# A convolution moved into four quarters of the TensorE array, with 56-token blocks, three-slot units and three PSUM banks for the front

## Chip, cores, metric

One core of a Trainium2 chip. The time is device microseconds (us) of one execution. Every experiment was timed beside the kernel before on the same chip, in the same rounds; different jobs got different chips, and that turned out to matter (the kernel before has a median of 725.5 us on one and 622.8 to 624.2 on three others). In the profile's lines PE is TensorE (PEld its weight loads), DVE VectorE, ACT ScalarE, POOL GpSimd and SP SyncE, which issues most of the loads; a q behind the name is that engine's sequencer, and L101 is line 101 of the kernel. "Ratio" is the mean time of one kernel's fast runs over that of the kernel before in the same rounds, so not quite the ratio of the medians quoted.

## The reference

```python
# x: 8 x 3584 x 192 fp32 (28,672 tokens); weight: 8 heads x 7 taps
w = softmax(weight)                                   # per head
y[t] = sum_k w[head, k] * x[t - 6 + k]                # causal, zero-padded per sequence
logits = y @ w_gate;  e = argmax(logits)              # 8 experts, top 1
g = softmax(logits)[e];  o = sigmoid(y @ w_output_gate)[e]
out = g * o * (relu(y @ w1[e]) @ w2[e])               # 192 -> 1024 -> 192
```

## The kernel before

Tokens go through in 16 units of 1,792. The *front* of a unit loads x, does the convolution as a matmul with a band matrix, transposes, computes the gate, and scatters the rows, sorted by expert, to a stream in HBM. The *slots* read 512 rows of one expert back (two transposing DMAs, xa and xb) and do the two expert matmuls. In the main loop unit u runs four slots while the front of unit u+2 is laid between them. The parts the change touches:

```python
BT = 112; KI = BT + 6                                  # block of 112 tokens, 118 rows with history
def load_x(u):
    ...
    nc.sync.dma_start(xt[0:BT, c0:NB, :], src(c0, NB - c0, 0, BT))      # 112 partitions
    nc.sync.dma_start(xt[BT:KI, c0:NB, :], src(c0, NB - c0, BT, KI))    # 6 partitions
...
def front_a(u):
    for h in range(H):                                 # one head a step, whole array
        pc = pft()
        nc.tensor.matmul(pc[0:BT, 0:NB * GH], band[0:KI, h, :], xt[0:KI, :, h*GH:(h+1)*GH], ...)
        evac(cv[0:BT, :, h*GH:(h+1)*GH], pc[...])
        yield
    if ahead and u + 2 < NU: xts[u + 2] = load_x(u + 2)
...
for u in range(U0, NU):                                # main loop
    while k < len(todo):                               # slots
        for q in range(4):
            pos = 4 * k + q
            if 0 <= 16*(u-U0) + pos - 4 < 16: load_w(1)      # expert weights, one piece
            ... s.first / front steps / prev.second ...
            if pos == 7 and u + 1 < NU: nxt = loads(u + 1)   # slot loads of the next unit
```

## Time and profile before

| | us |
|---|---|
| timed, median of 3 (range) | 719.81 (716.82 to 725.0) |
| the profiled execution (span) | 622.8 (621.1) |
| TensorE busy in that span | 575.6, 93% |
| a unit in the steady part | 36.7 |
| a full slot of 512 rows, TensorE alone | 5.65 |

TensorE is busy almost without a gap in the steady part (35.9 of the 36.6 us of a unit), so the span there is the sum of its work; the lines that show it are in the prediction. Two more lines of the page, in 40 equal slices of the span, are the granted TensorE clock in tenths, and the mean busy share of the 16 DMA engines in tenths.

```profile
PEclk9999989999999999999999999999999999989997
DMA  6999759993847365464635647354463425256631
```

### The profile page before, as it was taken

Reading aid. Unit: us, or ns where it says so; the run is one execution under the profiler, and the core shown is the slowest. Engines: PE = TensorE matmul, PEld = TensorE weight load, DVE = VectorE, ACT = ScalarE, POOL = GpSimd, SP = SyncE. Lnnn points to the kernel's source line nnn. Section 1 sums busy time; section 2 is a strip of 40 time slices with the busy share of each in tenths; the row PEclk is TensorE's granted clock in tenths of the full one; section 3 lists DMA queues with packets and bytes.
Section 4 is the critical chain, followed back from the end, with each engine's and each line's share of the span. In section 5 each row is a group of like instructions: output and inputs, shape, how many; then the busy total and the mean of one; then the engine's idle time right before and its main releaser. Section 6 shows DMA issues by size and latency. Waiting matters only on the chain.

```text
span 621.1 us, 13578 instructions
## 1 busy us (share of the span) xinstructions
PE 575.6 (93%) x4544; PEld 359.2 (58%) x4544; DVE 380.4 (61%) x1310; ACT 381.8 (61%) x638; POOL 403.5 (65%) x419
## 2 busy tenths in 40 slices
PE   3999689999999999999999999999999999989992
PEld 1555346665665756566565665666566665646561
DVE  7678664856739476584946658385674948526231
ACT  1677555675666656576575656667566666746761
POOL 1378538777766757576575766747576675775774
PEclk9999989999999999999999999999999999989997
DMA  6999759993847365464635647354463425256631
GB/s 159 203 198 258 184 112 195 157 254 109 194 115 154 128 119 173 109 182 98 164 110 115 177 103 187 88 133 142 114 180 95 103 90 110 80 124 129 186 107 37
DMA packets 162569, 88.13 MB, mean 142 GB/s; under 512 B 116766, under 2 KB 153793, under 8 KB 162497
## 3 DMA queue, kind: packets, MB, share of 16 engines
q1 hardware_dynamic: 131872, 43.92, 32.0%
q0 software_dynamic: 29728, 43.30, 26.5%
q8 instruction: 36, 0.59, 0.4%
q14 instruction: 37, 0.29, 0.2%
q10 hardware_dynamic: 896, 0.03, 0.1%
HBM read 35.92 MB, written 43.06 MB: 127 GB/s over the span
## 4 chain that ended last, share of the span: by engine, by line
PE 80%; DVE 7%; ACT 5%; DMA 4%; issue 2%; POOL 1%; ACTq 0%; SPq 0%; POOLq 0%; DVEq 0%
PE pyt L668 22%; PE pp L626 18%; PE pf L303 12%; PE pp L633 10%; PE pf L457 6%; PE pf L317 6%; PE pf L326 4%; ACT ht L646 3%; DVE ht L644 2%; PE pf L335 1%; ACT cv L291 1%; DMA out_dram<-y,oi 1%; DMA xb<-xcg_sorted 1%; DVE np L382 1%; DVE xrow L422 1%
## 5 line engine op out<-in xcount | busy, mean ns | idle before, releaser
L495 POOL DMA_INDIRECT out_dram<-y,oi x246 | 244.7, 995 | 121.4 <-ACT y L674 57.1
L646 ACT ACTIVATE ht<-pp 128x1024 f16<-128x1024 f32 (+1 forms) x189 | 182.9, 1001 | 57.7 <-PE pp L633 56.7
L668 PE MATMUL pyt<-wres,ht 128*128 128x192 f16 x1920 | 191.4, 246 | 0.0
L668 PEld LDWEIGHTS <-ht 128*128 128x128 f16 x1968 | 167.4, 98 | 24.4 <-issue 10.9
L475 POOL DMA_INDIRECT xcg_sorted<-xs,du x128 | 133.3, 1042 | 72.4 <-ACT xs L291 31.7
L644 DVE TENSOR_SCALAR ht<-pp 128x1024 f16<-128x1024 f32 (+1 forms) x63 | 75.4, 1198 | 73.6 <-PE pp L626 73.6
L303 PE MATMUL pf<-xt,band 118*112 118x384 f32 x256 | 104.9, 504 | 11.0 <-DMA wg<-n_moe_w_output_gate_dram 10.6
L626 PE MATMUL pp<-xa,wres 128*128 128x512 f16 x240 | 93.2, 388 | 4.9 <-DMA xa<-xcg_sorted 4.8
L626 PE MATMUL pp<-xb,wres 128*128 128x512 f16 x240 | 91.5, 381 | 2.2 <-DMA xb<-xcg_sorted 2.2
L291 ACT CAST xs<-pf 128x388 f16<-128x388 f32 x128 | 61.6, 485 | 49.7 <-PE pf L457 47.9
L674 ACT COPY y<-pyt 128x384 f32<-128x384 f32 x123 | 58.4, 475 | 36.2 <-PE pyt L668 33.5
L633 PE MATMUL pp<-xa,wres 64*128 64x512 f16 x240 | 73.1, 385 | 0.0
L633 PE MATMUL pp<-xb,wres 64*128 64x512 f16 x240 | 73.1, 385 | 0.0
L626 PEld LDWEIGHTS <-wres 128*128 128x128 f16 x480 | 33.8, 97 | 66.9 <-issue 62.7
L457 PE MATMUL pf<-xrow,pm 112*128 112x194 f16 x512 | 64.5, 247 | 7.4 <-ACT cv L291 4.0
L457 PEld LDWEIGHTS <-pm 112*128 112x128 f16 x512 | 44.9, 97 | 34.5 <-issue 12.3
L427 DVE TENSOR_SCALAR pm<-pos,pos 112x256 f16<-112x256 f16 x256 | 62.6, 305 | 0.0
L422 DVE TENSOR_TENSOR xrow<-cv,gs 112x384 f16<-112x384 f32 x121 | 61.9, 550 | 0.0
L303 PEld LDWEIGHTS pf<-xt,band 118*112 118x112 f32 x256 | 41.6, 182 | 26.5 <-DVE band L142 11.0
L293 DVE COPY cv<-pf 112x384 f32<-112x384 f32 x48 | 26.5, 551 | 42.9 <-PE pf L303 42.8
L291 ACT COPY cv<-pf 112x384 f32<-112x384 f32 x80 | 38.0, 478 | 21.6 <-PE pf L303 21.0
L317 PE MATMUL pf<-identf,cv 112*128 112x112 f32 x384 | 49.3, 259 | 0.7 <-ACT cv L291 0.7
(135 smaller groups left out, 432.2 us busy)
## 6 DMA issues: line engine op xcount, KB each, us to landing
xt<-in_x_dram SPq DMA_DIRECT2D x8, 1344.0 KB
xt<-in_x_dram SPq DMA_DIRECT2D x8, 1260.0 KB
out_dram<-y,oi POOLq DMA_INDIRECT x246
wres<-in_moe_w_dram POOLq DMA_DIRECT2D x8, 384.0 KB
wd<-wres SPq DMA_DIRECT2D x3, 768.0 KB
wres<-in_moe_w_dram POOLq DMA_DIRECT2D x8, 256.0 KB
xcg_sorted<-xs,du POOLq DMA_INDIRECT x128
xcg_sorted<-zrow SPq DMA_DIRECT2D x8, 256.0 KB
```

Of the source, the lines that this page charges most:

```text
L291: nc.scalar.copy(out=o, in_=i)
L303: nc.tensor.matmul(pc[0:BT, 0:NB * GH], band[0:KI, h, :], xt[0:KI, :, h * GH:(h + 1) * GH], start=True, stop=True)
L317: nc.tensor.matmul(pt[:, j * BT:(j + 1) * BT], cvf[0:BT, m * 2 * D + i * 128:m * 2 * D + (i + 1) * 128], identf[0:BT, 0:BT], is_transpose= ...
L422: nc.vector.tensor_tensor(out=xr[P, k:k + 2, 0:D], in0=cv[P, k:k + 2, :], in1=gs[P, k:k + 2].unsqueeze(2).to_broadcast([BT, 2, D]), op=ALU ...
L457: nc.tensor.matmul(ps[:, r * XW:(r + 1) * XW], pm[P, l, r * 128:(r + 1) * 128], xr[P, l * NG + i, :], start=(r == 0 and l == 0), stop=(r = ...
L475: i = nc.gpsimd.indirect_dma_start(out=xcg2, out_offset=bass.IndirectOffsetOnAxis(ap=du[:, i:i + 1], axis=0), in_=xs.rearrange("p r w -> p ...
L495: i = nc.gpsimd.indirect_dma_start(out=out, out_offset=bass.IndirectOffsetOnAxis(ap=oi[:, j:j + 1], axis=0), in_=y[:, j, :], in_offset=Non ...
L626: nc.tensor.matmul(pps[r][:, l, :], w[:, o2:o2 + 128], x, start=(r == 0), stop=(r == 1))
L633: nc.tensor.matmul(pps[r][:, l, :], w[p0:p0 + 64, c:c + 128], x[p0:p0 + 64], start=(r == 1), stop=(r == 0))
L644: nc.vector.tensor_relu(out=ht, in_=pps[r])
L646: nc.scalar.activation(out=ht, in_=pps[r], func=AF.Relu)
L668: nc.tensor.matmul(self.pp[:, o:o + D], self.ht[fc // 2][:, fc % 2, q * 128:(q + 1) * 128], self.w[:, w:w + D], start=(fc == 0 and q % 2 = ...
```

## The change

Its intent: take TensorE time away. A 64x64 quarter of the array gets a block of 56 tokens with 6 rows of history (62 partitions); four quarters multiply together. In five of the units three slots run instead of four, and the remaining rows go to slots picked at the end. The front gets three PSUM banks (PSUM is the memory that the kernel's matmuls write to: pf, pp and pyt in the profile's lines), the second matmul keeps one. Weights start earlier. The core (helpers, names and the rest of the placement cut):

```diff
-    BT = 112
-    KI = BT + PADL
+    BH = 56
+    KH = BH + PADL                 # 62
+    PT = 64 + BH                   # 120 partitions, 8 of them dead
@@ load_x
-        nc.sync.dma_start(xt[0:BT, c0:NB, :], src(c0, NB - c0, 0, BT))
-        nc.sync.dma_start(xt[BT:KI, c0:NB, :], src(c0, NB - c0, BT, KI))
+        nc.sync.dma_start(xt[0:KH, c0:NB, :], src(c0, NB - c0, 0))
+        nc.sync.dma_start(xt[64:64 + KH, :, :], src(NB, NB, 0))
@@ pools
-    ps_y bufs=2   ps_f bufs=2
+    ps_y bufs=1   ps_f bufs=3
@@ front_a
-        for h in range(H):
-            pc = pft()
-            nc.tensor.matmul(pc[0:BT, 0:NB * GH], band[0:KI, h, :], xt[0:KI, :, ...])
+        for h in range(0, H, 2):
+            pcs = [pft(), pft()]
+            for hh in range(2):
+                for r, c in ((0, 0), (1, 1), (0, 1), (1, 0)):
+                    nc.tensor.matmul(pcs[r][64*c:64*c+64, ...], band[64*r:64*r+KH, h+hh, :],
+                                     xt[64*r:64*r+KH, c*NG:(c+1)*NG, ...])
@@ plan
-        p = plan_half(u % 2, "a")                       # four experts a unit
+        n = 3 if u in (4, 6, 8, 10, 12) else 4 if u < NU - 1 else E
@@ weights
-    load_w(8)          # before the first front; 8 more in the prologue, 16 in the loop
+    load_w(12)         # much earlier; 4 + 16 in the loop
```

## The prediction

> **What bounds the kernel now.** I read the page first: engine shares, the 40 slices, the chain that ended last, then the timeline of TensorE in the steady part, then the chain in order of time, and last the DMA issues.
>
> ```profile
> span 621.1 us, 13578 instructions
> ## 1 busy us (share of the span) xinstructions
> PE 575.6 (93%) x4544; PEld 359.2 (58%) x4544; DVE 380.4 (61%) x1310; ACT 381.8 (61%) x638; POOL 403.5 (65%) x419
> ...
> PE 80%; DVE 7%; ACT 5%; DMA 4%; issue 2%; POOL 1%; ACTq 0%; SPq 0%; POOLq 0%; DVEq 0%
> ```
>
> TensorE is busy 93% and owns 80% of the chain; the others have a third of their time free. The timeline of TensorE in the middle shows why: no gaps, one stage following the other.
>
> ```profile
> 303.75 0.82 PE L303 MATMUL pf<-xt,band 118*112 118x384 f32 x2
> 304.41 0.50 PE L457 MATMUL pf<-xrow,pm 112*128 112x194 f16 x4
> ...
> 327.24 1.71 PE L326 MATMUL pf<-tt,wg 128*32 128x448 f32 x16
> 328.88 0.39 PE L626 MATMUL pp<-xa,wres 128*128 128x512 f16 x1
> ```
>
> The columns are start, length, engine, line. One head of the convolution (L303) holds TensorE from 303.75 to 304.41, so 0.65 us; a unit of 1792 tokens has 8, so 5.2 us. The gating matmuls of a unit (L326: four column tiles of 32, twice, fp32) take 1.64 us to the next stage. The chain in order of time gives the period: the same L326 piece stands at 290.65, 327.31 and 363.98.
>
> ```profile
> 290.65 1.64 PE pf L326 x16
> ...
> 327.31 1.64 PE pf L326 x16
> ...
> 363.98 1.64 PE pf L326 x16
> ...
> 537.41 1.32 PE pyt L668 x16
> ...
> 540.24 1.32 PE pyt L668 x16
> ...
> 543.07 1.32 PE pyt L668 x16
> ```
>
> A unit is 36.67 us, all TensorE. After the last front, half an expert slot takes 2.83 us, so a full slot of 512 rows 5.65 us, and four of them are 22.6 of the 36.67.
>
> The x loads hide behind this. The input of each unit comes in two DMAs, one of 112 partitions and one of 6:
>
> ```profile
> xt<-in_x_dram SPq DMA_DIRECT2D x8, 1344.0 KB
> xt<-in_x_dram SPq DMA_DIRECT2D x8, 1260.0 KB
> ...
> xt<-in_x_dram SPq DMA_DIRECT2D x8, 72.0 KB
> xt<-in_x_dram SPq DMA_DIRECT2D x8, 67.5 KB
> ```
>
> In the trace the first unit's 1,888 packets of 768 bytes move between 2.3 and 10.3 us, with about 16 packets in flight and 36 to 45 ns a packet on an engine; the first convolution starts at 10.6. There is one thing outside the profile: the timed median is 719.8 us against 622.8 for the profiled execution. The profile doesn't show these 97 us; I carry them along as a constant.
>
> [...] the four column tiles of L326 start at 327.242, .249, .255 and .262 and each holds its tile for a 0.38 us pass, and the step into or out of a tiled stage costs about 0.09 us (a matmul at 304.96 of 512 columns would let the next start at 305.17; the row-tiled one starts at 305.27). No run here yet shows rows and columns tiled at once.
> [...] the semaphore of the first 112-partition load gets sixteen increments between 8.29 and 9.56 us; that of the 6-partition load one event at 3.26, long before any of it has landed, and then six, 9.46 to 10.31. So six partitions ran on six engines. [...]
> [...] Here the first matmul after a 3.1 us wait (L626 at 78.2 us) took 0.59 us instead of 0.38.
>
> **The change part by part.**
> *Convolution in quarters.* Instead of one fp32 matmul of 384 columns for a head there are four of 192 columns on 64x64 quarters. If the four run together as the tiles of L326 do, a head takes 0.33 instead of 0.65 us. Four steps of two heads: 8 x 0.33 + 4 x 0.19 (into and out of the tiling mode) = 3.4 instead of 5.2 us. Gain 1.8 us a unit.
> *Dead rows.* Tiles have 120 instead of 112 partitions, 8 of them dead. 24 transposes of 0.096 us and the gating matmuls grow by 7%: 0.16 + 0.11 = 0.27 us back. Net 1.5 us a unit; 12 units have their front in the steady part: 18 us.
> *Fewer slots.* Before: 13 x 4 + 8 = 60 full slots and 3 of half size. After: 8 x 4 + 5 x 3 + 8 = 55, plus 2 full and 4 half picked ones. I routed the inputs of the reference on paper: 29,180 rows, 57.0 full slots; both plans end with nothing left for the loop at the end. 3 full slots fewer and one half more: 3 x 5.65 - 3.1 = 13.9 us.
> *Three PSUM banks for the front, one for the second matmul.* The single bank must be copied out (0.475 us, L674) before the next two quarters of a slot; 1.5 us of first matmuls lie between. Nothing on the path, perhaps some tenths. The number and size of evictions stay (8 of 384 columns a unit).
> *Start.* The mask band is built for 2 heads of 56 columns first instead of 4 of 112 (seven copies of 0.66 us now), so it is ready some 3 us earlier, worth something only if x is there.
> *The x loads.* This is the part that I think decides. A block is now 62 rows (56 + 6), and each unit is loaded by two DMAs of 62 partitions x 16 blocks; the split at 112, which kept the big DMA on 16 engines, is gone. [...] each of the two runs on two engines[...]. A unit is 2 x 62 x 16 = 1,984 packets, 992 an engine. At 36 ns (the shortest that the trace has for this size with few in flight, too) that is **35.7 us a unit** instead of about 7.
>
> What follows step by step: x(0) lands at 2 + 36 = 38 us, x(1) at about 77, x(2) 115, x(3) 153, x(4) 190, each queued behind the last. The loads of slots share the queue, in order, and each spans all 16 engines, so they wait behind x on those two. The main loop starts near 200 us (79 before), and iteration 3, whose slots queue behind x(5) and x(6), near 275. From there a cycle forms: x(u+4) is issued when conv(u+2) is through, at a third to half of iteration u (about 14 us), needs 36 us and some 4 for other packets on the two engines, and the slots of iteration u+1 are queued behind it and need 4 more: 14 + 40 + 4 = 58 us an iteration instead of 36.7. Nine such iterations (3 to 11): 522 us, so 797. Then no x is left to load: iterations 12 to 14 about 30 + 36 + 24, the last with 8 slots and the picked ones 57, the end 18: 165. Sum 962 us of span, and with the 97 about 1,060 timed; the gains in TensorE time vanish in its waits. With 51 us an iteration (34 ns a packet, little interference) it is 890 and 990 timed, with 65 us 1,025 and 1,120.
>
> **Rivals.**
> *A: the loads spread well after all* [...]. For: the code around the first unit is tuned as if x came at 10 us[...]. Then TensorE stays the bound: 621 - 18 - 13.9 - about 6 at the start = 583 us, 680 timed, 5 to 6% faster. Other engines can take it: a three-slot unit would be 29.5 us, and ACT, which has 23.5 us of work in a four-slot unit, would have 19.5, DVE 21.5 of 23.
> *B: quarters don't overlap in fp32.* With only two at a time the conv gains nothing and pays 0.76 us of mode changes and 0.27 of dead rows a unit: 621 + 12 - 14 = 619, no change. Against it: L326 overlaps four. Alone it would show only under A.
> *C: two engines, but in the shadow.* If x merely had to keep pace with the unit (35.7 against 35.1), the kernel would be about even. Against it: the start alone loses 27 us for x(0) and as much again for each of the next units, and 16 x 35.7 = 571 us must pass before conv(15), which has 120 us behind it today: 690 is the least, without one packet of another kind on those engines, which in this trace carry 280 us more each.
>
> **Range and chances.** 0.80 for two engines, nearly all of it slower by far: centre 1,050, 850 to 1,150 for how much waits overlap. 0.20 for A or B, mostly faster: 0.17 faster, 0.03 within 2%. The range covers the first branch alone; that is a little under 8 in 10, and I don't stretch it over the empty middle.
>
> **What would show it.** Right: the first convolution starts after 35 us and waits for a DMA of xt; the 62-partition loads have two late semaphore increments each; DMA share of the 16 engines falls to some 0.3 while two are full; TensorE is idle half of the middle and its clock drops below 0.95; each period is 50 to 65 us. In the convolution itself the four quarters start within 30 ns and a two-head step takes about 0.75 us. Wrong: the first convolution before 15 us and sixteen increments a load: then A holds, and I read the 680. If quarters start one after the other, the tiling step is wrong. If slots wait for scatters rather than x, the cycle is misread.

## The result

| | median us (range, runs) | span of the profiled run | mean clock |
|---|---|---|---|
| before, same rounds | 722.22 (716.82 to 725.0, 4) | | |
| after | 1185.03 (1182.35 to 1195.68, 4) | 1184.5 | 0.777 |

The ratio is 1.645 (1.630 to 1.660). The kernel became much slower, for the reason predicted; the time is above the range.

The page of the kernel after: TensorE's share, clock, DMA share, the chain that ended last, and the x loads.

```profile
span 1184.5 us, 14837 instructions
...
PE 621.3 (52%) x5200; PEld 373.8 (32%) x5200; DVE 391.4 (33%) x1367; ACT 362.1 (31%) x618; POOL 394.7 (33%) x424
...
PEclk9985767596579586887859677786859778898997
DMA  5311223535155321424243322424233243235631
...
PE 16%; SPq 12%; another core or an unknown queue 4%; DMA 4%; issue 4%; DVE 2%; POOL 1%; ACT 1%; POOLq 0%; DVEq 0%; ACTq 0%
...
xt<-in_x_dram SPq DMA_DIRECT2D x24, 744.0 KB
```

TensorE fell from 93% to 52% busy. The chain's shares can't be compared with those of before: here they add up to 45% only, because the profile follows the chain back to 653 us and no further. In the part that it follows, SP's sequencer holds nearly as much (12) as TensorE (16); before it held 0. The DMA engines as a mean are a third busy (20.9% and 13.7% for the two large queue kinds), while the kernel waits for DMA: that is possible when a few of them carry what it waits for. What TensorE waits for says the same (line waited for, us in total, times, longest):

```profile
PE pp L677 <- DMA xa<-xcg_sorted: 319.1, 11, 64.8
PE pf L330 <- DMA xt<-in_x_dram: 135.0, 7, 38.1
```

For 62 rows the prediction's two engines were an estimate that its trace didn't show; this one does. The semaphore of the first x load (62 partitions of 15 blocks) has one event at 2.21 us and then two, at 34.71 and 37.93; the second has its two at 59.84 and 62.42. And of the 768-byte packets 1.7 are in flight as a mean between 4 and 34 us, where the kernel before, with sixteen increments for its 112 rows, has 16.9 between 4 and 8. So two engines each. A cycle of the steady part, in the chain in order of time (start, us, what):

```profile
704.64 0.27 SPq L101
704.95 18.96 SPq L102
...
724.79 20.99 SPq L633
...
745.92 4.62 DMA xb<-xcg_sorted
...
753.10 1.49 PE pf L330 x16
```

L101 and L102 issue the two x loads of a unit. The second holds SP's sequencer for 19 us, and the transposing slot load behind it (L633) holds it for 21 more; the slot's rows land at 750.5, the convolution starts at 753.1, and only when it is through does the next x load go out. I had expected the slots to land late, not the issuing engine to stand still; the effect is the same order of events.

The marks of nine such cycles: from the issue of x to the first matmul of the slots queued behind it 47.4 us as a mean (43.9 to 53.0), from there to the next issue of x 21.9 us (19.2 to 23.8). Convolution starts: 341.6, 413.2, 482.9, 548.0, 617.5, 683.6, 753.0, 822.0, 889.0, 962.6, so 69.0 us a cycle.

### The profile page after: what moved, and what is told of

The parts are those of the page before. It is cut to its first block, busy times and chain, and to the rows that moved or that the text cites. A ratio compares the mean times of both kernels' runs of the same rounds, so it can differ in the third digit from the quotient of the medians.

```text
span 1184.5 us, 14837 instructions
## 1 busy us (share of the span) xinstructions
PE 621.3 (52%) x5200; PEld 373.8 (32%) x5200; DVE 391.4 (33%) x1367; ACT 362.1 (31%) x618; POOL 394.7 (33%) x424
## 3 DMA queue, kind: packets, MB, share of 16 engines
q1 hardware_dynamic: 130432, 46.82, 20.9%
q0 software_dynamic: 29248, 43.29, 13.7%
## 5 line engine op out<-in xcount | busy, mean ns | idle before, releaser
L535 POOL DMA_INDIRECT out_dram<-y,oi x236 | 234.8, 995 | 308.8 <-ACT y L725 247.6
L317 DVE COPY cv<-pf 120x384 f32<-120x384 f32 x48 | 26.7, 555 | 393.6 <-PE pf L330 355.8
L330 PE MATMUL pf<-xt,band 62*64 62x192 f32 x1024 | 75.6, 407 | 139.3 <-DMA xt<-in_x_dram 135.0
L330 PEld LDWEIGHTS pf<-xt,band 62*64 62x64 f32 x1024 | 44.0, 164 | 172.1 <-issue 134.2
L315 ACT COPY cv<-pf 120x384 f32<-120x384 f32 x80 | 37.0, 483 | 197.8 <-PE pf L330 167.0
L351 PE MATMUL pf<-identf,cv 120*128 120x120 f32 x384 | 62.9, 297 | 35.2 <-DVE cv L317 18.2
L497 PE MATMUL pf<-xrow,pm 120*128 120x194 f16 x512 | 68.9, 256 | 17.4 <-DVE pm L467 8.2
L351 PEld LDWEIGHTS pf<-identf,cv 120*128 120x128 f32 x384 | 48.6, 159 | 46.3 <-DVE cv L317 20.2
L462 DVE TENSOR_TENSOR xrow<-cv,gs 120x384 f16<-120x384 f32 x122 | 62.4, 551 | 0.0
L467 DVE TENSOR_SCALAR pm<-pos,pos 120x256 f16<-120x256 f16 x256 | 61.7, 293 | 0.0
```

The lines of the kernel that those rows point to most:

```text
L315: nc.scalar.copy(out=o, in_=i)
L330: nc.tensor.matmul(pcs[r][64 * c:64 * c + 64, hh * NG * GH:(hh + 1) * NG * GH], band[64 * r:64 * r + KH, h + hh, :], xt[64 * r:64 * r + KH ...
L351: nc.tensor.matmul(pt[:, j * PT:(j + 1) * PT], cvf[0:PT, m * 2 * D + i * 128:m * 2 * D + (i + 1) * 128], identf[0:PT, 0:PT], is_transpose= ...
L497: nc.tensor.matmul(ps[:, r * XW:(r + 1) * XW], pm[P, l, r * 128:(r + 1) * 128], xr[P, l * NG + i, :], start=(r == 0 and l == 0), stop=(r = ...
L535: i = nc.gpsimd.indirect_dma_start(out=out, out_offset=bass.IndirectOffsetOnAxis(ap=oi[:, j:j + 1], axis=0), in_=y[:, j, :], in_offset=Non ...
```

## The experiments

Fifteen kernels in four jobs. Median of the kernel before: 725.5 in the first job, 624.2, 622.8 and 623.6 in the others, four different chips. e0, e2, e3, e7 and e14 were run once, so whether they ran in the fast state is unknown; the differences read from e2, e3, e7 and e14 are far larger than the spread of repeated runs. Each job had one chip, so what is called a chip's property below could also be the job's.

### First job: what the loads cost, and what the 97 us are

**e0_before**: no edit.

> The kernel before, unchanged, for its own profile beside its times. Its profile on record has 622.8 us, its timed runs 717 to 725 us, and the changed kernel shows no such gap (profiled 1186.4, timed 1182 to 1196). Theory 1: a slower granted clock of TensorE in the timed runs; then this profile shows about 720 us with a clock well below the 0.985 of the first profile, and matmuls of 192 columns spaced wider than 0.082 us. Theory 2: a fixed launch cost outside the span; then the span is 622 again beside a time of 720, and the changed kernel should have had it too, which it has not.

724.9 us, span 723.1, clock 0.938. The span is the time, so nothing lies outside the profile: the launch theory falls. The first profile of the kernel before was of another, faster kind of execution than its timed runs. Both run alike to 134 us; then one has units of 36.7 us, the other of about 43.6. Two stretches of one unit each of the slow one, and two of the first profile (start and end, length, busy us of each engine, then clock, DMA share, GB/s):

```profile
254.90:297.30 42.40, 38.45 (x292) 23.46 (x291) 23.34 (x79) 23.07 (x39) 23.85 (x25) 0.96 0.46 116
297.30:341.70 44.40, 39.47 (x292) 23.95 (x291) 24.32 (x80) 23.04 (x38) 23.92 (x25) 0.92 0.45 117
```

```profile
290.60:327.20 36.60, 35.89 (x291) 22.71 (x290) 23.93 (x79) 22.92 (x37) 24.01 (x25) 1.00 0.54 133
327.20:363.90 36.70, 35.99 (x292) 22.73 (x290) 23.39 (x78) 23.65 (x38) 24.10 (x25) 1.00 0.54 138
```

By these lines TensorE idles 4.0 and 4.9 us of a slow unit and 0.7 of a fast one, and is busy 2.6 to 3.5 us longer: about half of the 7 us is idle time, the other half slower work. The clock record of the slow one shows a half-clock window of 3.4 or 6.8 us in nearly every unit; in the first profile there is none between 83 and 551 us. The later jobs settle whose property it is, as far as runs can: all 21 of their runs of the same kernel took 621.8 to 625.8 us, all 7 of the first job's 718 to 731. It goes with the chip or the job, not with the execution. Why TensorE stops and the clock halves once a unit there stays open; of TensorE's semaphore updates the trace holds 758 where its instructions have 867 (862 in the first profile), so the gaps at these windows can't be read to their cause.

**e1_split48**: each 62-row load cut in two.

```diff
-        nc.sync.dma_start(xt[0:KH, c0:NB, :], src(c0, NB - c0, 0))
-        nc.sync.dma_start(xt[64:64 + KH, :, :], src(NB, NB, 0))
+        for q0, q1 in ((0, 48), (48, KH)):
+            nc.sync.dma_start(xt[q0:q1, c0:NB, :], src(c0, NB - c0, q0, q1))
+            nc.sync.dma_start(xt[64 + q0:64 + q1, :, :], src(NB, NB, q0, q1))
```

> The changed kernel with each load of 62 partitions cut in 48 + 14, nothing else. Theory (two DMA engines for 62 partitions): [...] a unit's x lands in 7 to 10 us, the first convolution starts before 15 us, the conv and slot gains come out: 0.93 to 0.97 of the kernel before. Rival (quarters that do not overlap, the single bank of the second matmul, or the new order of slots made it slow): it stays above 1.2 times the kernel before.

777.07 us, ratio 1.073 (1.057 to 1.089), clock 0.901. Same bytes, same packets, 408 us less than the kernel after. But it is still 7% slower than before, so the gains didn't come.

**e2_before118**: the kernel before, its two loads of 112 and 6 partitions made one of 118.

```diff
-        nc.sync.dma_start(xt[0:BT, c0:NB, :], src(c0, NB - c0, 0, BT))
-        nc.sync.dma_start(xt[BT:KI, c0:NB, :], src(c0, NB - c0, BT, KI))
+        nc.sync.dma_start(xt[0:KI, c0:NB, :], src(c0, NB - c0, 0, KI))
```

> The kernel before with its two x loads of 112 and 6 partitions joined to one of 118 = 2 x 59, nothing else. Theory: two engines, 944 packets each of 40 to 54 ns, 38 to 51 us a unit; 1000 to 1250 us in all, two late increments of the load's semaphore. Rival (the load is not what costs): 620 to 740 us.

910.2 us: 185 us from this one line in a kernel that has nothing else of the change. Right in kind, less than expected. Its packets took 36 to 45 ns, and x(0) and x(1) were used at 44.6 and 75.7 us.

**e3_split31**: as e1, cut at 31, so two halves of 31 rows.

> The changed kernel with each load of 62 partitions cut in 31 + 31. [...] each half runs on one engine, the same for all four DMAs, so 1,984 packets one after the other, 71 to 107 us a unit, 1500 to 2200 us in all. Rival rule (partitions spread over 16 engines, rounded up, and something else slow about 62): 31 behaves as 62, about 1185 us or less.

1655.6 us. With loads of 31 rows the time is 2.3 times that of before, with 62 1.65, with 48 and 14 1.07. The semaphores go with it: the first loads of 31, 62, 118 and 48 rows have 1, 2, 2 and 16 late increments. Those of 6, 56 and 112 rows in the kernels before and after have 6, 14 and 16. In these seven sizes the count is the largest divisor of the rows that is at most 16; for other sizes of the x loads it was not read.

### Second job: where the expected gains went

These ran on a chip where the kernel before takes 624. The expectations count in the first chip's 725, so they are to be read as ratios to it.

**e4_fullconv**: the kernel after with the convolution back on the whole array and loads of 112 and 6; everything else of the change kept. (Edit: load_x, band and matmul as before, two heads a step.)

> The changed kernel with the convolution put back on the whole array (112-token blocks, x in loads of 112 and 6 partitions, no dead rows), everything else of the change kept: three-slot units, picked slots, one bank for the second matmul, three for the front, weights ahead, new order of the steps. The repaired kernel e1_split48 was 777 us against 725 for the kernel before. Theory N (the new schedule costs the 7%): this run stays at 760 to 800. Theory Q (the quarters cost it, with their two evictions at once and four loads a unit): this run has the 14 us of fewer slots as a gain and comes to 695 to 720.

635.96 us, ratio 1.018 (1.017 to 1.020): neither number. The slots gain in the steady part and the start loses, see the table in the next job.

**e5_quarters**: the kernel before with the quarters alone (the matmul lines of the diff above, loads as in e1_split48).

> The kernel before with the convolution in quarters alone (x in loads of 48 and 14 partitions twice, two heads a step, dead rows), its own schedule, slots and banks kept. Theory N: quarters are worth what the prediction counted, 1.5 us a unit, and this run is 695 to 720. Theory Q: 750 to 790.

641.0 us, ratio 1.028 (1.026 to 1.030). So neither theory: both halves of the change lose. By the table in the next job 14.5 of the 15.9 us that the span of this one loses lie before unit 6, and I did not take those apart. In the steady part it should gain and doesn't, because the quarters alone wait once in every unit. The timeline of TensorE there, then that of VectorE (start us, length us, engine, line):

```profile
242.09 0.38 PE L661 MATMUL pp<-xb,wres 128*128 128x512 f16 x1
242.40 0.54 PE L328 MATMUL pf<-xt,band 62*64 62x192 f32 x2
244.12 0.87 PE L328 MATMUL pf<-xt,band 62*64 62x192 f32 x14 [1.19 <-issue]
244.93 0.83 PE L703 MATMUL pyt<-wres,ht 128*128 128x192 f16 x8
```

```profile
243.74 0.28 DVE L474 SCALAR_TENSOR_TENSOR dd<-pf,rowf,dd 128x72 f32<-128x72 f32 x1
```

The first quarter starts at 242.40; the second, which writes the other bank, at 244.12. The page's word is "issue", but TensorE's sequencer stands in a wait on VectorE's semaphore that comes at 244.03, as L474 ends, the last reader of the routing's bank. A two-head step wants two banks at once, and this kernel has two in all. That is 1.7 us a unit against a gain of 1.5 (measured in e9_best4), and the unit is 36.8 us, as before.

**e6_banks**: the kernel before with the banks of the change alone.

```diff
-    ps_y bufs=2   ps_f bufs=2
+    ps_y bufs=1   ps_f bufs=3
```

> The kernel before with one PSUM bank for the second matmul and three for the front, nothing else. The prediction gave this some tenths of a microsecond at most: 715 to 735. If the copy out of the single bank (0.48 us, waited for 14.6 us in e1_split48) is what the repaired kernel loses by, 750 or more.

616.31 us, ratio 0.988 (0.986 to 0.991), a unit of 36.1 us. The prediction's "some tenths" is right. Whether the third bank is what the quarters need is tested in e9_best4. (The opposite test, the changed schedule with two front banks, wasn't run.)

**e7_split38**: the kernel after, its loads cut in 38 and 24 rows.

> The changed kernel with each 62-row load cut 38 + 24 instead of 62: [...] The two engines then carry 608 + 64 packets a unit instead of 992. If the packets on those two engines set the period (44 us for 992), it falls by 14 us, from 69 to 55, and with it the time to about 970 (930 to 1010). If it is rather that the queue is blocked for as long as any two-engine load is in it, the time stays above 1100.

872.4 us, and units of 49.5 us (six, 415.0 to 712.0). The expectation counts two engines for 38 rows and twelve for 24, so 672 packets on each of the two instead of 992: an estimate from the counts read in the first job, since the increments of this run were not read. The rival, a queue blocked for as long as any two-engine load is in it, falls. The packets on those two engines set the period, more strongly than I expected; the comparison on a chip of the same speed comes with the next run.

### Third job: the changed kernel on a fast chip, and repaired

**e11_after**: no edit.

> The changed kernel, unaltered, beside the kernel before on whatever chip this job gets. Before was 725 on the chip of the first job and 624 on that of the second. Theory C (the 97 us are a property of the chip, and the changed kernel, which waits for DMA most of the time, feels it less): on a chip where before is near 624 the changed kernel comes to 960 to 1060, ratio 1.55 to 1.7, and on one where before is near 720 to 1185 again. If its cycle of 69 us was the DMA's alone, it is 1150 to 1190 on any chip.

1122.3 us, ratio 1.795 (1.779 to 1.811), the profiled run 1118.1 with a span of 1116.1; before took 622.8. So between the two expectations: 63 us of its 1185 belong to the chip, where before loses 97. A cycle is 66.6 us here: 49.0 from the issue of x to the slots and 17.6 on to the next issue. The DMA part is as long as on the slow chip, only the TensorE part is shorter. Against e7_split38 a unit is 16.6 us longer (66.1 to 49.5) for 320 more packets an engine, by that estimate: 52 ns a packet, all of it on the path.

**e8_load64**: the kernel after with 64 rows a load, the last two unused.

```diff
-        nc.sync.dma_start(xt[0:KH, c0:NB, :], src(c0, NB - c0, 0))
-        nc.sync.dma_start(xt[64:64 + KH, :, :], src(NB, NB, 0))
+        nc.sync.dma_start(xt[0:64, c0:NB, :], src(c0, NB - c0, 0))        # 64 rows
+        nc.sync.dma_start(xt[64:128, :, :], src(NB, NB, 0))               # last unit: 48 + 14
```

> The changed kernel with 64 rows a load instead of 62 (the last two unused), nothing else[...]. Theory D (the two-engine loads are the whole catastrophe): the unit period comes down from 69 us to 33 to 36, the first convolution starts before 15 us, and the ratio to before is 0.99 to 1.05: the convolution's 1.5 us a unit and the fewer slots as gains, the later start of the main loop (e4_fullconv: 22 us) as loss. If the two-engine rule is not the cause, the ratio stays above 1.3.

638.9 us, ratio 1.026 (1.022 to 1.031). Two rows more a load take 483 us away. Theory D holds: this is the whole catastrophe. What remains is a change that loses 2.6% by itself.

**e9_best4**: the kernel before with quarters, the banks of e6_banks and 64-row loads; four slots a unit and the start of before, but for two pieces of the changed start that came along: the mask band is built for two heads first, and GpSimd clears the xs tiles.

> The kernel before with the quarters, one bank for the second matmul and three for the front, and 64-row loads; its own schedule of four slots a unit and its own start. Quarters alone (e5_quarters) lost 1.7 us a unit because two banks were wanted at once and only two were there; the banks alone (e6_banks) gained 0.55. If the stall was the banks, the unit is 36.1 - 1.5 + 0.3 = 34.9 us and the ratio 0.96 to 0.98. If quarters have another cost, 1.00 or more.

616.1 us, ratio 0.989 (0.986 to 0.992), a unit of 35.1 us from the fourth on. The unit is as expected, the ratio misses the 0.96 to 0.98: the table below has unit 6 come 5.6 us later than before. The wait for a bank is gone; one step in TensorE's timeline is now whole:

```profile
301.74 0.38 PE L664 MATMUL pp<-xb,wres 128*128 128x512 f16 x1
302.05 0.88 PE L331 MATMUL pf<-xt,band 62*64 62x192 f32 x16
302.87 0.50 PE L706 MATMUL pyt<-wres,ht 128*128 128x192 f16 x4
```

```profile
282.02 0.38 PE L654 MATMUL pp<-xb,wres 128*128 128x512 f16 x1
282.24 1.46 PE L312 MATMUL pf<-xt,band 118*112 118x384 f32 x4
283.53 0.66 PE L696 MATMUL pyt<-wres,ht 128*128 128x192 f16 x6
```

The second fence is the same step on the whole array, from e4_fullconv. From the start of the 512-column matmul before it (which lets the next start 0.21 us later) to the start of the matmul after it, two heads take 1.12 us in quarters and 1.51 on the whole array, so 0.91 and 1.30 without those 0.21. Four steps: 1.5 us a unit.

**e10_three**: the kernel after with 64-row loads and the start of the kernel before (8 weight pieces first, gate weights from ScalarE's queue, its steps of the prologue).

> The changed kernel with 64-row loads and the start of the kernel before: weights loaded in its order (8 pieces first, not 12), the gate weights on ScalarE's queue, the fronts of the prologue in its steps, four steps of the next routing ahead of the loop. If the order of the start is what the changed schedule lost by (22 us in e4_fullconv), this is 20 us below e8_load64 and the fastest of all, ratio 0.95 to 0.98. If not, it equals e8_load64 within 6 us.

619.8 us, ratio 0.995 (0.991 to 0.998). As expected 19 us below e8_load64, but not the fastest: with two and a half slots less it is slower than e9_best4. The table cuts the spans of the fast-chip profiles at the gating matmuls of unit 6 and unit 15.

| kernel | to unit 6 | unit 6 to 15 | rest | span, us |
|---|---|---|---|---|
| before | 180.6 | 330.0 | 110.5 | 621.1 |
| e6_banks | 180.2 | 325.0 | 108.6 | 613.8 |
| e5_quarters | 195.1 | 331.4 | 110.5 | 637.0 |
| e9_best4 | 186.2 | 315.8 | 109.9 | 611.9 |
| e4_fullconv | 200.0 | 315.5 | 118.7 | 634.2 |
| e8_load64 | 195.7 | 320.8 | 121.3 | 637.8 |
| e10_three | 183.2 | 314.5 | 120.2 | 617.9 |

The last column but one shows the picked slots: 8 to 11 us more. The middle should show four to five slots fewer, 23 to 28 us; from e9_best4 to e10_three it shows 1.3, and on the whole array, from e6_banks to e4_fullconv, 9.5. Two stretches of one four-slot and one three-slot unit of e10_three, and two units of e9_best4:

```profile
323.20:360.90 37.70, 33.91 (x315) 20.66 (x314) 23.77 (x76) 20.84 (x34) 21.22 (x22) 0.95 0.61 142
360.90:393.90 33.00, 31.75 (x320) 20.38 (x321) 24.03 (x79) 21.04 (x35) 23.05 (x24) 1.00 0.55 132
```

```profile
291.50:326.60 35.10, 34.65 (x340) 22.02 (x338) 24.09 (x79) 22.71 (x38) 23.61 (x25) 1.00 0.61 144
326.60:361.70 35.10, 34.66 (x340) 22.03 (x338) 23.61 (x78) 23.36 (x38) 23.62 (x25) 1.00 0.65 146
```

70.7 us for seven slots and 70.2 for eight. TensorE idles 5.0 us in the first pair and 0.9 in the second, and after the longest wait runs 3.4 us at half clock. What it waits for in the first pair:

```profile
PE pp L679 <- DMA xa<-xcg_sorted: 2.3, 1, 2.3
PE pf L416 <- DVE msk L409: 1.2, 1, 1.2
PE pp L679 <- DMA xb<-xcg_sorted: 0.8, 1, 0.8
PE pf L499 <- DVE pm L469: 0.7, 1, 0.7
```

By the code, the unit after a three-slot one issues its scatters up to quarter step 10 instead of 7 and only then the slot loads for the next, so that 5 instead of 8 steps are left for the rows to come back.

### Fourth job: two things still open

**e12_spread**: e9_best4 with the loop's 16 weight pieces over 24 quarter steps.

```diff
-                if 0 <= 16 * (u - U0) + pos - 4 < 16:
+                if 16 * (u - U0) + pos in {0, 2, 3, 5, 6, 8, 9, 11, 12, 14, 15, 17, 18, 20, 21, 23}:
                     load_w(1)
```

> e9_best4 with the 16 weight pieces of the main loop issued over 24 of its quarter steps instead of 16 in a row, nothing else. In e9_best4 a unit takes 35.1 us from the fourth on, but the third takes 42.0: the first slots of the next one come 3.9 us late, and the clock then halves for 6.8 us. The DMA engines are at 1.1 to 1.2 busy between 100 and 140 us. If the burst of weights delays the rows' way out and back, the third unit comes down to 36 to 38 us and the ratio to before to 0.975 to 0.985. If the rows are late because the unit is shorter, it stays at 0.989.

610.9 us, ratio 0.979 (0.977 to 0.982), the fastest of all. The third unit of the loop takes 37.4 instead of 42.0 us, the wait is 1.6 instead of 3.9. The rest of the profile isn't as clean: the loop's first unit takes 41.2 us instead of 36.2, with a wait of 6.2 us for its rows, and 2.7 us are gained before the loop and 2.1 after unit 15. So the ratios show that spreading helps; the sum of the stages doesn't divide it up. **e13_banks_spread** is the control.

> e6_banks (whole-array convolution, one and three banks) with the same spread of the weight pieces: a control. It has no such wait, so nothing changes: ratio 0.985 to 0.991. If spreading helps it as much as e12_spread, the effect isn't about the quarters.

617.3 us, ratio 0.989 (0.987 to 0.992): no effect without the quarters. So the burst of weights made the long third unit.

**e14_two_early**: e10_three with the two 62-row loads of the kernel after.

> e10_three with the 62-row loads of the changed kernel, so two engines again, but with the weights loaded late in the start (8 pieces first, later than x(0)). In the changed kernel a 768-byte packet took 59 ns in the first 36 us, with the weights moving, and the first unit was there at 62 us instead of the predicted 38. If the weights on those two engines do that, the first unit is there at 42 to 48 us here, and the whole time is 20 to 60 us below the changed kernel's 1122 (1185 on a chip where before is near 720). If the packets are as slow without them, at 58 us or later.

1101.8 us; the second half of the first unit is used at 58.4 us, 61.3 in e11_after. The packets took 60 ns in the first 38 us here too. But the edit didn't do what it was meant to: GpSimd issues the first eight weight pieces at 15.7 to 20.4 us, where e11_after and the kernel after have them at 14.9 to 19.5, so the run doesn't test the weights. The trace of the kernel after does: before 14.5 us no weight has moved, and its packets take 59 ns there as well. So for the first 14.5 us the weights are refuted; for the rest it is open. The number of engines isn't it either: in e8_load64, where the first convolution starts at 8.6 us instead of 38.1, so that its x loads have more than two (with two, the 960 packets of the first at 59 ns would take 28 us), the packets take 59 ns in the first 38 us. Why a 62-row load starts with 60 ns a packet, while one of 118 rows on two engines (e2_before118) has 36 to 45 from the start, stays open.

## Why the prediction was wrong

The mechanism was right; the steps that failed are the time of a packet and with it the length of an iteration and of the start, the end, and a constant that wasn't one.

**Right: what decides.** "x loads on two engines" and the ratio's direction. Expected signs that came: first convolution at 38.1 us (after 35), two late semaphore increments a load, mean DMA share 0.35 (20.9% and 13.7% for the two queue kinds), TensorE idle half of the time, clock 0.777, four quarters starting within 20 ns. Signs that were missed: the period (69.0 us, not 50 to 65) and the two-head step (0.91 us at full clock, not 0.75). For the number of engines the trace of the prediction had shown only 112 partitions with sixteen increments and six with six; the runs now show 62, 118, 31 and 48 (2, 2, 1 and 16). Its claim that the slots queue behind x holds as well, with the measured numbers of the chain above (the first slot load of the kernel before has sixteen increments, 77.96 to 78.09 us). Rival A (loads spread anyway) is out by e8_load64, B (quarters don't overlap) by the timeline of e9_best4, C (in the shadow) by the first unit at 62 us.

**Wrong: the size.** The sum was 275 us to iteration 3, nine cycles of 58, and 165: 962 us of span. Measured in the profile: 341.6, 9 x 69.0, and 221.9, together 1184.5. The 222 us that are missing are 66 + 99 + 57; the 97 us carried along hid nearly half of them.

- *"At 36 ns" a packet.* The two engines' packets took 59 ns up to 38 us, 43 to 62, 54 to 90, 48 to 110, 39 to 200 and 44 from there to 1,000. Over the whole run the mean is 44 ns, and the trace from which the 36 were read has a mean of 45 for the same packets: 36 is its median (its shortest is 34). With 45 the sum would have come closer here; in e2_before118, also on two engines, the mean is 38. x(0) was complete at 62 and x(1) at 111 instead of 38 and 77; x(2) and x(3) then followed after 37 and 38 us, as predicted. That is 34 of the 66 us of the start. The other 32 fall between unit 3 and unit 5, in the loop's first iteration: from its first slot matmul (232.4) to that of iteration 3 (338.5) it takes 106 us, where the sum had 75 (200 to 275). x(5) and x(6), issued at 242.2 and from 265.7 us, go out one after the other there, ahead of the slots.
- *"14 + 40 + 4 = 58 us an iteration".* The 40 + 4 measured 47.4, so 3 us of the 11. The 14 measured 21.9: 8 us. On the fast chip this part took 17.6. There TensorE has idled 24 to 42 us when the rows arrive and starts at half clock: in e11_after the first eight matmuls of a slot take 3.2 us (from 737.16) and the next eight 1.6, the first two-head step 1.5 and the others 0.8; that is 2 to 3 of the 3.6 us, and the rest would be a 14 that was short at full clock. In the kernel after it is the same, one step of a unit at half clock and the others as in e9_best4:

```profile
753.03 1.56 PE L330 MATMUL pf<-xt,band 62*64 62x192 f32 x16
...
758.18 0.88 PE L330 MATMUL pf<-xt,band 62*64 62x192 f32 x16
```

  The other 4.3 us belong to the record's chip, most of them to every second cycle: there the next x goes out 7.2 us after the start of the last two-head step, where e11_after has 1.0. At 696.96 us such a step starts and is over at 697.8 by its records, but VectorE and ScalarE, which wait for it, start to copy at 704.2, and x is issued then. It looks like the stop of e0_before, whose cause stays open.
- *The end*, "last 165": 221.9 on this chip, 180.1 for the same stretch on the fast one, where the sum was only 15 short.
- *"I carry them along as a constant."* The 97 us are not outside the profile and not a constant: they go with another chip or job. Where before takes 622.8, the kernel after takes 1122 (the profiled run has a span of 1116), 154 above the 962. That 1122 would lie inside the range is luck, since the range has the 97 in it. The 154 are 62 at the start, 77 in the cycles, 15 at the end.

**Wrong without being seen, under rival A:** had the loads been right, I expected 583 us of span; e8_load64 has 637.8. The convolution gained 1.5 us a unit (1.8 before the dead rows expected; 0.91 us a step, where the sum had 0.85 and the list of signs 0.75), and the steady unit 1.0 net of the dead rows (36.1 to 35.1; expected 1.5). The slots gained 1.3 us in the steady part beside the quarters (9.5 without them) of the 23 to 28 that their number is worth, and 8 to 11 went into the picked slots at the end. The waits above took the place of the rest: "fewer slots" was counted as TensorE time in a schedule whose rows come back 2 us too late. And the start was expected 6 us earlier and came later: e8_load64 reaches unit 6 at 195.7 against 180.6, and 183.2 with the start of before (e10_three), so 12.5 of these 15 us are the new order of the start.

## What to carry to other kernels

Check the partition count of every load when a tile size changes: 62 rows for 64 made 639 us into 1122, with no more bytes to move. A profile and a time can be of different chips; before a difference between them is carried along, measure both on one. And when a TensorE-bound loop is shortened, follow the data that must make a round trip within it, for here they didn't shorten with it (70.7 us for seven slots in e10_three, of which TensorE waits 3.1 for rows; 70.2 for eight in e9_best4), and spreading a burst of other transfers gave back more (0.989 to 0.979 of before) than the slots that were saved.

## What the runs show beside this, and what they leave open

- Loads on few engines: 62 and 118 partitions have two late increments, 31 one (1655.6 us), 48 sixteen; with 64 the kernel takes 638.9 us. On two engines 768-byte packets took 59 ns at the start and 44 as a mean, and the kernel 1122 us instead of 639.
- SP stood 19 us in the issue of one 62-row load and 21 in the transposing load behind it. What sets how long it is held, no run shows.
- The half-clock windows in the traces of the kernels before and after are multiples of 3.4 us (3.4 and 6.8 before, 3.4 to 64.9 after), but for those that the end of the trace cuts. On the chip where the kernel before had such a window in nearly every unit TensorE idled 4 to 5 us in the two units shown; what stopped it there, with 723 us of span, and not on the others, with 621, no run shows.
- Four quarters in fp32 do run together (a step's four start within 20 ns). What it costs to go in and out of them was not measured apart; it is part of the 0.91 us a step here against 0.65 for half of the whole-array step.
